# Attention scores and weight folds as 64x32 products, with the heads ordered even first

## The chip, the core and the metric

The kernel runs on one core of a Trainium2 chip. TensorE (PE in the profile, PEld for its weight loads) multiplies and writes to PSUM; VectorE (DVE) and ScalarE (ACT) read PSUM and do everything elementwise; GpSimd (POOL) clears buffers and reduces over partitions; SyncE (SP) issues most transfers. The metric is the device time of one execution in microseconds (us), as the median over runs. A profiled execution gives the trace, in which each instruction has a start and a duration.

## The reference, cut to what matters

Inputs are `q`, `k`, `v` of 8 batches x 8 heads x 576 positions x 64 and `phi` of 8 x 8 x 576 x 32, all float32, and two weight matrices. The computation is

```python
a = exp(phi - max(phi, axis=2)); a = a / (sum(a, axis=2) + 1e-9)
k_m = einsum('bhsm,bhsd->bhmd', a, k)            # 32 memory slots for each head
v_m = einsum('bhsm,bhsd->bhmd', a, v)
attn = softmax(q @ k_m.T / 8)                    # 576 x 32 for each head
x = (attn @ v_m), heads side by side             # 4608 tokens x 512
h = x @ w_in                                     # 512 -> 2048
out = (h * cos(h)) @ w_out                       # 2048 -> 512
```

## The kernel before

The kernel never forms `x`. For each batch it multiplies `v_m` into `w_in` once (a **fold**, giving a matrix `vw` of 256 x 2048: 8 heads x 32 slots), and then computes `h` as `attn @ vw`. All large products are done as three fp16 products of high and low halves.

**Main stream.** The 4608 tokens are cut into 12 groups of 384, and each group runs 16 steps `f` over 128 of the 2048 hidden columns. A step has `gemm1` (line 493, `hp<-aT,vw`: six products for 384 tokens, or twelve for 192 tokens in a group that straddles two batches), an elementwise chain for `h*cos(h)` (ACT lines 502, 512, 518, DVE lines 507, 508, 516, 519), and `gemm2` (line 537, `acc<-wo,gp`: nine products of 128x512) of the step five before. There are 192 steps; group 0 and half of group 1 also convert weights.

**Side stream.** For each batch `b` a generator, `prep(b)`, is advanced a few yields per step. `memory(b)` takes `exp(phi - max)`, multiplies it with `k` and `v` (`psA`, line 247, five chunks of positions, eight float32 products of 32 columns each), divides by the sum, transposes (`tpx`, line 267), and copies the result to two zero-filled tiles, `km` (ACT, lines 274 and 275) and `vm` (DVE, lines 276 and 277), in which two heads stand side by side as a block diagonal. `attend(b)` computes the **scores** (`sc`, line 349) in three blocks of 256, 256 and 64 positions, transposes each on DVE (line 351), takes the softmax, and transposes back. A separate list of due steps runs the folds: for each batch eight of them, (q, g) with q = 0..3 and g = 0, 1, two steps apart; from the third batch on a fold is four 128x32 products with `vp` (fp16 high halves of `vm`, both weight halves under each other) and four with `vl` (low halves, zeros where the other head stands), line 432, and then one ACT and one DVE instruction (lines 438, 439) that write `vw`.

**What sets the order.** The program text gives dependencies and priorities; a scheduler decides the static order of each engine's instructions. Each engine then works strictly through its own list, and waits where an operand is missing. Every small product (psA, tpx, sc, pv) takes its PSUM bank from a pool of two, `small_ps`, in turn; a bank is taken again when its readers are done. `hp` and `acc` have three banks each.

Of the kernel before, what the change touches and what calls it, by code (L numbers as in the profile page):

```python
# [9 lines left out]
F16 = mybir.dt.float16  # L10
# [12 lines left out]
P = 128  # L23
# [21 lines left out]
def attention_then_ffn(ctx: ExitStack, tc: tile.TileContext, phi, phiT, kv, qT, w_in, w_out, eye, out):  # L45
# [13 lines left out]
    nc.sync.dma_start(out=ident, in_=eye)  # L59

    vmask = const.tile([P, 2, 2], F32, name="vmask")
    nc.vector.memset(vmask, 0.0)
# [9 lines left out]

    vl = const.tile([P, NP, 2, M], F16, name="vl")
    nc.vector.memset(vl, 0.0)

# [138 lines left out]
    def memory(b):  # L214
# [28 lines left out]
        for c, (s0, n) in enumerate(TCH):  # L243
            for g in range(2):
                for j in range(4):
                    h = 4 * g + j
                    nc.tensor.matmul(  # L247
                        psA[32 * j:32 * (j + 1), g * KV:(g + 1) * KV],
                        lhsT=a[:n, c, h * M:(h + 1) * M], rhs=kvs[c][:n, h * KV:(h + 1) * KV],
                        start=(c == 0 and g == 0), stop=(c == 4), skip_group_check=True)  # L250
            yield
        if b >= 1 and b + 1 < B and b + 1 != 2:
# [13 lines left out]
        for g in range(2):  # L266
            nc.tensor.matmul(tpx[:, g * P:(g + 1) * P], lhsT=X[:, g], rhs=ident, start=True, stop=True)
        km = wk.tile([P, NP, 2 * M], F32, tag="km", name=f"km_{b}", bufs=1)
        vm = wk.tile([P, NP, 2 * M], F32, tag="vm", name=f"vm_{b}")
        nc.gpsimd.memset(km, 0.0)  # L270
        nc.gpsimd.memset(vm, 0.0)
        tv = tpx[:, 0:HM].rearrange("p (c t m) -> p c t m", t=2, m=M)
        lo, hi = slice(0, D), slice(D, P)
        nc.scalar.mul(km[lo, :, 0:M], tv[lo, :, 0], 1.0 / math.sqrt(D))
        nc.scalar.mul(km[hi, :, M:2 * M], tv[hi, :, 1], 1.0 / math.sqrt(D))
        nc.vector.tensor_copy(out=vm[hi, :, 0:M], in_=tv[hi, :, 0])
        nc.vector.tensor_copy(out=vm[lo, :, M:2 * M], in_=tv[lo, :, 1])
        st["km", b], st["vm", b] = km, vm
        yield
        l1 = wk.tile([P, 4], F32, tag="l1", name=f"l1_{b}")  # L280
        nc.vector.tensor_reduce(out=l1, in_=X.rearrange("p g (t d) -> p (g t) d", t=2), op=ALU.add, axis=AX.X,
                                apply_absolute_value=True)
        nc.vector.tensor_tensor(out=l1, in0=l1, in1=vmask.rearrange("p g t -> p (g t)"), op=ALU.mult)
        l2 = wk.tile([P, 1], F32, tag="l2", name=f"l2_{b}")
# [13 lines left out]
    def scales(b):  # L298
# [5 lines left out]
        if b < 2:  # L304
            T = wk.tile([P, 1], F32, tag="T", name=f"T_{b}")
            nc.vector.reciprocal(out=T, in_=E)
            nc.vector.tensor_scalar(out=T, in0=T, scalar1=2.0 ** 13, scalar2=None, op0=ALU.mult)
            st["T", b] = T
        else:

            sv = to_range(f"sv_{b}", wk, "sv", st["ev", b])
            vp = wk.tile([P, NP, 2, M], F16, tag="vp", name=f"vp_{b}", bufs=1)
            for o in range(2):
                here, there = slice(o * D, (o + 1) * D), slice((1 - o) * D, (2 - o) * D)
                vm = st["vm", b][here, :, (1 - o) * M:(2 - o) * M]
                nc.scalar.activation(vp[here, :, o], vm, AF.Copy, scale=sv[here])
                nc.scalar.activation(vp[there, :, o], vm, AF.Copy, scale=sv[here])
                nc.vector.scalar_tensor_tensor(out=vl[here, :, o], in0=vm, scalar=sv[here], in1=vp[here, :, o],
                                               op0=ALU.mult, op1=ALU.subtract)
            st["vp", b] = vp  # L320
# [3 lines left out]
    def attend(b):  # L324
# [95 lines left out]

    def fold_psum(b, q, g):
        pv = small_ps(f"pv_{b}_{q}_{g}")
        for i in range(2):
            c = 2 * g + i
            if b < 2:
                nc.tensor.matmul(pv[D * i:D * (i + 1)], lhsT=st["vm", b][:, c],
                                 rhs=w_in_sb[:, c, q * FS:(q + 1) * FS], start=True, stop=True)
        if b >= 2:
            for first in (True, False):
                for j in range(4):  # L430
                    c, o = 2 * g + j // 2, 1 - j % 2
                    nc.tensor.matmul(pv[M * j:M * (j + 1)], lhsT=(st["vp", b] if first else vl)[:, c, o],  # L432
                                     rhs=st["w2", q][:, c, o], start=first, stop=not first, skip_group_check=True)
        return pv
# [7 lines left out]
    def fold(b, q, g):  # L442
        if g == 0:
            st["vw", b, q] = wk.tile([P, 2, 2, FS], F16, tag="vw", name=f"vw_{b}_{q}", bufs=8)
        split_fold(b, st["vw", b, q], g, fold_psum(b, q, g))

# [292 lines left out]
```

## Time and profile before

| | |
|---|---|
| median of 3 runs | 719.82 us (718.49 to 720.54) |
| profiled execution | 718.65 us |
| its span (first to last instruction) | 716.6 us |
| PE busy | 694.8 us, 97% of the span |
| DVE busy | 570.0 us, 80% |
| ACT busy | 520.8 us, 73% |
| granted TensorE clock | 0.99 |

A row of a group reads: line, engine, operation, output<-inputs, shapes and count, then busy time and mean duration of one, then the engine's idle time before them and what ended it. A row of the timeline reads: start, duration until the end of the last one, engine, line, operation, count, and in brackets the idle time before it. Matmuls are pipelined: one of 512 columns is listed with 0.38 us, but the next starts 0.216 us after it. So the cost of a piece of work on PE is read from the distance between starts, not from durations.

### The profile page before, as it was taken

To read this page: it belongs to the slowest core of one execution; us is meant where nothing else is said; L and a number is where in the kernel's file an instruction comes from. 1 tells how busy PE (TensorE), PEld (TensorE's weight loads), DVE (VectorE), ACT (ScalarE), POOL (GpSimd) and SP (SyncE) were. 2 spreads that over 40 slices of the span, in tenths; PEclk is the share of its full clock that TensorE was granted. 3 is DMA by queue.
4 is the path that set the end of the run, shared out by engine and by line. 5 is a ranking of instruction groups with operands and counts; after the bars stand their busy time and mean duration, and the time that the engine had idled before them with its cause. 6 is when DMAs were issued, how large, how long until landed. Compare 5 with 4: busy or idle time off the path is not lost.

```text
span 716.6 us, 12018 instructions
## 1 busy us (share of the span) xinstructions
PE 694.8 (97%) x4578; PEld 357.2 (50%) x4578; DVE 570.0 (80%) x1256; ACT 520.8 (73%) x965; POOL 14.1 (2%) x34
## 2 busy tenths in 40 slices
PE   7689999999999999999999999999999999999997
PEld 3244444565454445565444544666444544555553
DVE  2868999998988997679877997679776987676753
ACT  1789999899886875668757685678767785665653
POOL 0000000000000000000000100000000000000000
PEclk9799999999999999999999999999999999999999
DMA  8995881426405300152103310152100000100101
GB/s 291 381 330 168 310 291 42 121 60 188 149 7 161 111 1 1 45 167 67 45 1 123 107 49 1 45 167 68 44 1 1 22 24 1 45 1 1 45 0 45
DMA packets 31561, 66.78 MB, mean 93 GB/s; under 512 B 2192, under 2 KB 11024, under 8 KB 31504
## 3 DMA queue, kind: packets, MB, share of 16 engines
q1 hardware_dynamic: 27184, 58.15, 25.1%
q10 hardware_dynamic: 4320, 7.87, 2.9%
q8 instruction: 36, 0.59, 0.3%
q14 instruction: 21, 0.17, 0.1%
HBM read 52.38 MB, written 9.44 MB: 86 GB/s over the span
## 4 chain that ended last, share of the span: by engine, by line
PE 60%; ACT 17%; DVE 16%; DMA 4%; issue 2%; SPq 1%; POOL 0%; ACTq 0%; DVEq 0%
PE acc L537 34%; PE hp L493 18%; PE pv L432 3%; ACT u L512 2%; DVE u L516 2%; DMA phi<-in_phi 2%; DVE u L508 2%; DVE gp L519 2%; ACT u L502 2%; ACT L512 2%; DVE gp L507 1%; DMA kv<-in_kv 1%; PE sc L349 1%; ACT L237 1%; PE psA L247 1%
## 5 line engine op out<-in xcount | busy, mean ns | idle before, releaser
L537 PE MATMUL acc<-wo,gp 128*128 128x512 f16 x1584 | 371.2, 379 | 0.0
L537 PEld LDWEIGHTS <-gp 128*128 128x128 f16 x1584 | 153.4, 98 | 161.5 <-issue 2.6
L493 PE MATMUL hp<-aT,vw 128*128 128x192 f16 (+1 forms) x1440 | 202.6, 284 | 0.8 <-DVE u L516 0.4
L493 PEld LDWEIGHTS <-vw 128*128 128x128 f16 x1440 | 125.1, 98 | 82.3 <-issue 30.0
L512 ACT ACTIVATE u<-u 128x384 f32<-128x384 f32 x192 | 99.7, 522 | 86.6 <-DVE u L508 85.7
L516 DVE SCALAR_TENSOR_TENSOR u<-hp,u 128x384 f32<-128x384 f32 x176 | 96.8, 552 | 45.7 <-ACT u L512 43.4
L502 ACT ACTIVATE u<-hp,cu 128x192 f32<-128x192 f32 (+1 forms) x240 | 110.3, 491 | 18.2 <-PE hp L493 11.8
L519 DVE TENSOR_TENSOR gp<-u,gp 128x384 f16<-128x384 f32 x176 | 96.6, 551 | 29.9 <-ACT gp L518 29.3
L518 ACT CAST gp<-u 128x384 f16<-128x384 f32 x176 | 89.0, 509 | 38.7 <-DVE u L516 36.7
L508 DVE TENSOR_TENSOR u<-u,gp 128x384 f32<-128x384 f32 x192 | 105.7, 552 | 3.2
L507 DVE CAST gp<-u 128x384 int32<-128x384 f32 x192 | 67.4, 353 | 20.6 <-ACT u L502 18.9
L532 PE MATMUL acc<-wo,gp 128*128 128x512 f32 x96 | 45.5, 603 | 1.6 <-DVE gp L514 1.6
L439 DVE SCALAR_TENSOR_TENSOR vw<-pv,vw 128x512 f16<-128x512 f32 x48 | 33.0, 689 | 5.1 <-ACT vw L438 3.8
L438 ACT ACTIVATE vw<-pv 128x512 f16<-128x512 f32 x48 | 28.3, 590 | 7.4 <-PE pv L432 6.5
L484 PE MATMUL hp<-aT,vf 128*128 128x384 f32 x64 | 26.4, 546 | 4.2 <-DVE gp L514 2.0
L512 ACT ACT_TABLE_LOAD x23 | 29.5, 1283 | 0.4
L532 PEld LDWEIGHTS acc<-wo,gp 128*128 128x128 f32 x96 | 17.0, 190 | 20.7 <-issue 14.9
L247 PE MATMUL psA<-kv,phi 128*32 128x129 f32 (+1 forms) x640 | 23.5, 276 | 2.8 <-DMA kv<-in_kv 1.5
L553 ACT ACTIVATE ob<-acc,os 128x512 f32<-128x512 f32 x28 | 18.5, 682 | 8.1 <-PE acc L537 5.2
L247 PEld LDWEIGHTS psA<-kv,phi 128*32 128x32 f32 (+1 forms) x640 | 16.1, 109 | 13.3 <-issue 6.9
L484 PEld LDWEIGHTS hp<-aT,vf 128*128 128x128 f32 x64 | 12.5, 207 | 17.7 <-DVE gp L514 4.6
L349 PE MATMUL sc<-q,km 128*64 128x256 f32 (+3 forms) x192 | 20.6, 343 | 0.0
(126 smaller groups left out, 549.5 us busy)
## 6 DMA issues: line engine op xcount, KB each, us to landing
kv<-in_kv SPq DMA_DIRECT2D x32, 516.0 KB, 5.8
q<-in_qT SPq DMA_DIRECT2D x8, 1152.0 KB, 6.4
raw_out<-in_w_out SPq DMA_DIRECT2D x8, 1024.0 KB, 5.0
out<-ob ACTq DMA_DIRECT2D x30, 256.0 KB, 2.1
raw_in<-in_w_in SPq DMA_DIRECT2D x6, 1024.0 KB, 8.4
phi<-in_phi SPq DMA_DIRECT2D x8, 512.0 KB, 7.2
w_in_sb<-w_in_parts SPq DMA_DIRECT2D x12, 256.0 KB, 4.1
phiT<-in_phiT SPq DMA_DIRECT2D x4, 576.0 KB, 6.4
```

What stands on the lines that cost most here:

```text
L247: nc.tensor.matmul(psA[32 * j:32 * (j + 1), g * KV:(g + 1) * KV], lhsT=a[:n, c, h * M:(h + 1) * M], rhs=kvs[c][:n, h * KV:(h + 1) * KV], s ...
L484: nc.tensor.matmul(hp[:, :GT], lhsT=st["vf", q][:, g, fo * P:(fo + 1) * P], rhs=st["aTf"][:, g], start=(g == 0), stop=(g == 1))
L493: nc.tensor.matmul(hp[:, c0:c0 + n], lhsT=vw[:, wi, g, fo * P:(fo + 1) * P], rhs=aT[:, ai, g, c1:c1 + n], start=(k == 0), stop=(k == 5))
L502: ins = nc.scalar.activation(u[:, c0:c0 + n], hp[:, c0:c0 + n], AF.Copy, scale=st["cu", b] if grp else 1.0 / (2.0 * math.pi), bias=0.25)
L507: nc.vector.tensor_copy(out=ni, in_=u)
L508: nc.vector.tensor_tensor(out=u, in0=u, in1=ni, op=ALU.subtract)
L512: nc.scalar.activation(u, u, AF.Sin, scale=TWO_PI_BELOW)
L516: nc.vector.scalar_tensor_tensor(out=u, in0=hp[:, :GT], scalar=2.0 ** -17, in1=u, op0=ALU.mult, op1=ALU.mult)
L518: nc.scalar.copy(gp[:, 0], u)
L519: nc.vector.tensor_tensor(out=gp[:, 1], in0=u, in1=gp[:, 0], op=ALU.subtract)
L532: nc.tensor.matmul(accs[grp][t], lhsT=gp[:, t * P:(t + 1) * P], rhs=wo[:, f + 1], start=(f == 0), stop=(f == NF - 1))
L537: nc.tensor.matmul(accs[grp][t], lhsT=gp[:, gi, t * P:(t + 1) * P], rhs=parts[:, wi], start=(f == 0 and gi == 0 and wi == 0), stop=(f == N ...
```

## The change

Batches are counted from 0. From the third on (b >= 2) four things differ.

1. The host puts the even heads first and the odd heads behind them (`k`, `v`, `phi`; `q` and the weights stay), and swaps key and value columns for the second half instead of for odd heads. After the transpose all even heads' keys stand in the lower 64 partitions and all odd heads' in the upper 64, so `km` and `vm` are dense (4 x 32 columns) and need no zeros and no memset. Their four copies are written in the order ACT, DVE, ACT, DVE.
2. The scores are eight products of 64 rows x 32 columns for each block, the even heads' into one bank and the odd heads' into the other, with two DVE transposes, where there were four products of 128x64 into one bank with one transpose.
3. A fold of q does both g at once, into both small banks: eight 128x32 products with `vp`, then eight 64x32 products with `vl`, which has lost its zeros. Then the two pairs of ACT and DVE instructions follow.
4. The five psA chunks of a batch come without a yield between them, so the generator has four yields fewer and what follows is emitted sooner. The l1 norm of the values needs no mask.

```diff
+            if b < 2 or c == 4:
                 yield
...
+        n = 2 * M if b < 2 else M
+        km = wk.tile([P, NP, n], F32, tag="km", name=f"km_{b}", bufs=1)
+        vm = wk.tile([P, NP, n], F32, tag="vm", name=f"vm_{b}")
+        if b < 2:
+            nc.gpsimd.memset(km, 0.0)
+            nc.gpsimd.memset(vm, 0.0)
...
+        else:
+            tv = tpx[:, 0:HM].rearrange("p (g j m) -> p g j m", g=2, m=M)
+            for g in range(2):
+                nc.scalar.mul(km[HALF[g]], tv[HALF[g], g], 1.0 / math.sqrt(D))
+                nc.vector.tensor_copy(out=vm[HALF[1 - g]], in_=tv[HALF[1 - g], g])
...
         def scores(i):
             t0, n = BL[i]
+            if b >= 2:
+                sc = [small_ps(f"sc_{b}_{t0}_{g}") for g in range(2)]
+                for j in range(4):
+                    for g in range(2):
+                        nc.tensor.matmul(sc[g][M * j:M * (j + 1), :n], lhsT=km[HALF[g], j],
+                                         rhs=qt[HALF[g], j, t0:t0 + n], start=True, stop=True)
+                for g in range(2):
+                    nc.vector.transpose(at[:, 2 * t0 + g * n:2 * t0 + (g + 1) * n], sc[g][:, :n])
+                return
...
-        if b >= 2:
-            for first in (True, False):
-                for j in range(4):
-                    c, o = 2 * g + j // 2, 1 - j % 2
-                    nc.tensor.matmul(pv[M * j:M * (j + 1)], lhsT=(st["vp", b] if first else vl)[:, c, o],
-                                     rhs=st["w2", q][:, c, o], start=first, stop=not first, skip_group_check=True)
+    def fold_16(b, q):
+        pv, w2 = [small_ps(f"pv_{b}_{q}_{g}") for g in range(2)], st["w2", q]
+        for g in range(2):
+            for j in range(4):
+                nc.tensor.matmul(pv[g][M * j:M * (j + 1)], lhsT=st["vp", b][:, j, 1 - g], rhs=w2[:, j, 1 - g],
+                                 start=True, stop=False, skip_group_check=True)
+        for j in range(4):
+            for g in range(2):
+                v = HALF[1 - g]
+                nc.tensor.matmul(pv[g][M * j:M * (j + 1)], lhsT=vl[v, j], rhs=w2[v, j, 1 - g],
+                                 start=False, stop=True, skip_group_check=True)
...
+        elif g == 0:
+            for x, pv in enumerate(fold_16(b, q)):
+                split_fold(b, st["vw", b, q], x, pv)
```

What the scheduler makes of it is seen in three places. The first is PE at the scores of the last batch (`sc_<block>` before, `sc_<block>_<g>` now; 64x256 and 32x256 are output rows by positions). Before:

```order
L537 MATMUL acc_2_5474<-wo,gp_13_5751 128x512
L349 MATMUL sc_0_5977<-q_5229,km_5894 64x256 x4
L349 MATMUL sc_256_5983<-q_5229,km_5894 64x256 x4
L493 LDWEIGHTS vw_0_5444
L493 MATMUL hp_3_5989<-aT_5106,vw_0_5444 128x384
```

With the change:

```order
L370 MATMUL sc_0_0_5986<-q_5202,km_5894 32x256 x4
L532 LDWEIGHTS vw_0_5518
L532 MATMUL hp_1_6034<-aT_5061,vw_0_5518 128x384
L370 MATMUL sc_0_1_5987<-q_5202,km_5894 32x256 x4
L576 LDWEIGHTS gp_12_5802
L576 MATMUL acc_0_5557<-wo,gp_12_5802 128x512
L370 MATMUL sc_256_0_6010<-q_5202,km_5894 32x256 x4
L576 LDWEIGHTS gp_12_5802
L576 MATMUL acc_0_5557<-wo,gp_12_5802 128x512
L576 LDWEIGHTS gp_12_5802
L576 MATMUL acc_0_5557<-wo,gp_12_5802 128x512
L370 MATMUL sc_256_1_6011<-q_5202,km_5894 32x256 x4
```

Two blocks that stood together, in one small bank each, are now four halves with pieces of the main stream between them. Over batches 2 to 7 the order shows 7 of the 12 blocks of 256 cut into their two halves like this, and 5 with all eight products alternating between the halves; of the 6 blocks of 64, 4 are cut.

The second place is PE at the first fold of batch 4 (`vp` and `vl` are the high and low halves; of rows that repeat, one is shown). Before:

```order
L432 LDWEIGHTS vp_3590
L432 MATMUL pv_0_0_3598<-w_in_0_953,vp_3590 32x512
L432 LDWEIGHTS vl
L432 MATMUL pv_0_0_3598<-w_in_0_953,vl 32x512
L493 LDWEIGHTS vw_1_2711
L493 MATMUL hp_4_3609<-aT_2234,vw_1_2711 128x384
```

With the change:

```order
L462 MATMUL pv_0_0_3642<-w_in_0_952,vp_3634 32x512
L462 LDWEIGHTS vp_3634
L462 MATMUL pv_0_1_3643<-w_in_0_952,vp_3634 32x512
L467 LDWEIGHTS vl
L467 MATMUL pv_0_0_3642<-w_in_0_952,vl 32x512
L467 LDWEIGHTS vl
L467 MATMUL pv_0_1_3643<-w_in_0_952,vl 32x512
L532 LDWEIGHTS vw_1_2740
L532 MATMUL hp_4_3664<-aT_2147,vw_1_2740 128x384
```

Two folds (g = 0 and g = 1) that stood two steps apart are one stretch of sixteen products now, the last eight alternating between the two banks. Of the 24 stretches 20 stay whole; the first of batch 3, the second of batch 5 and the last of batches 4 and 6 are cut into two or three. The psA chunks of a batch stand together in batches 3 to 7 (four and one in batch 2); before, those of batches 2 to 7 stood in 18 places, 6 of them beside a fold, and now in 7, 2 of them beside a fold.

The third place is ACT at batch 4, from the end of the exponentials to the copies into `km`, with the semaphores waited for in brackets. Before, the two copies follow each other:

```order
L518 CAST gp_8_3121<-u_8_3120 128x384 [waits DVE_49]
L502 ACTIVATE u_9_3187<-hp_9_3174,cu_1945 128x192 [waits PE_49]
L502 ACTIVATE u_9_3187<-hp_9_3174,cu_2576 128x192
L274 ACTIVATE km_3209<-tpx_3206 64x4x32 [waits PE_49,Pool_49]
L275 ACTIVATE km_3209<-tpx_3206 64x4x32
L512 ACTIVATE u_9_3187<-u_9_3187 128x384 [waits DVE_49,Activation_49]
```

With the change:

```order
L551 ACTIVATE u_6_3092<-u_6_3092 128x384 [waits DVE_49,Activation_49]
L541 ACTIVATE u_7_3156<-hp_7_3143,cu_1959 128x192 [waits PE_49]
L541 ACTIVATE u_7_3156<-hp_7_3143,cu_2605 128x192
L557 CAST gp_5_3042<-u_5_3041 128x384 [waits DVE_49]
L557 CAST gp_6_3093<-u_6_3092 128x384 [waits DVE_49]
L473 ACTIVATE vw_3_3111<-pv_3_0_3112 128x512 [waits PE_49]
L473 ACTIVATE vw_3_3111<-pv_3_1_3113 128x512 [waits PE_49]
L551 ACTIVATE u_7_3156<-u_7_3156 128x384 [waits DVE_49,Activation_49]
L290 ACTIVATE km_3137<-tpx_3134 64x128 [waits PE_49]
L541 ACTIVATE u_8_3213<-hp_8_3200,cu_1959 128x192 [waits PE_49,Activation_49]
L290 ACTIVATE km_3137<-tpx_3134 64x128 [waits DVE_49]
```

The two copies into `km` are apart, the second waits for DVE's copy into `vm` between them, and both fold instructions of the last q stand ahead of them in one piece.

More of the change, by code (lines that the diff above doesn't have):

```diff
@@ L275, in memory @@
[L275 to L277 removed]
+        n = 2 * M if b < 2 else M
[4 more added lines that the diff above has]
+            nc.gpsimd.memset(vm, 0.0)
+        lo, hi = HALF
@@ L713 @@
     w_in, w_out = np.asarray(inputs["moe_w_in"]), np.asarray(inputs["moe_w_out"])
+    k, v, phi = k.copy(), v.copy(), phi.copy()
+    order = list(range(0, H, 2)) + list(range(1, H, 2))
+    for a in (k, v, phi):
+        a[2:] = a[2:, order]
     kv = np.ones((B, S, H, KV), k.dtype)
     kt, vt = k.transpose(0, 2, 1, 3), v.transpose(0, 2, 1, 3)
-    kv[:, :, 0::2, 0:D], kv[:, :, 0::2, D:2 * D] = kt[:, :, 0::2], vt[:, :, 0::2]
-    kv[:, :, 1::2, 0:D], kv[:, :, 1::2, D:2 * D] = vt[:, :, 1::2], kt[:, :, 1::2]
+    for bs, even, odd in ((slice(0, 2), slice(0, H, 2), slice(1, H, 2)), (slice(2, B), slice(0, 4), slice(4, H))):
+        kv[bs, :, even, 0:D], kv[bs, :, even, D:2 * D] = kt[bs, :, even], vt[bs, :, even]
+        kv[bs, :, odd, 0:D], kv[bs, :, odd, D:2 * D] = vt[bs, :, odd], kt[bs, :, odd]
     laid = {
```

49 lines of the change are left out of this document (27 added, 22 removed).

## The prediction

> **What bounds the kernel now.** I read the page's first lines, then the windows, then the groups of PE.
>
> ```profile
> PE 694.8 (97%) x4578; PEld 357.2 (50%) x4578; DVE 570.0 (80%) x1256; ACT 520.8 (73%) x965; POOL 14.1 (2%) x34
> ```
> ```profile
> 200.00:300.00 100.00, 99.36 (x691) 49.15 (x690) 81.19 (x184) 72.75 (x139) 2.36 (x5) 1.00 0.18 58
> 400.00:500.00 100.00, 99.80 (x736) 54.86 (x735) 83.26 (x193) 73.77 (x144) 3.59 (x6) 1.00 0.21 70
> 500.00:600.00 100.00, 99.81 (x637) 47.66 (x635) 82.28 (x186) 73.30 (x136) 0.66 (x1) 1.00 0.04 17
> ```
> ```profile
> L537 PE MATMUL acc<-wo,gp 128*128 128x512 f16 x1584 | 371.2, 379 | 0.0
> L493 PE MATMUL hp<-aT,vw 128*128 128x192 f16 (+1 forms) x1440 | 202.6, 284 | 0.8 <-DVE u L516 0.4
> ```
>
> The windows give length, then busy time of PE, PEld, DVE, ACT, POOL, then the granted clock (1.00). Busy PE alone proves little, so the last two rows matter: before 3024 main products PE stood idle 0.8 us in all. The next product starts when the last one's columns have gone through, and nothing else is waited for. DVE has 17% to spare, ACT 26%. So from batch 2's work on (160 us) a microsecond of PE's list is a microsecond of the end, and the question is what the small products cost there, and whether PE still never waits.
>
> **What a small product costs on PE.** The critical chain gives nine main products their true length, the timeline the starts around the small ones.
>
> ```profile
> 594.25 1.94 PE acc L537 x9
> ```
> ```profile
> 432.54 2.10 PE L537 MATMUL acc<-wo,gp 128*128 128x512 f16 x9
> 434.57 0.40 PE L432 MATMUL pv<-w_in,vp 128*32 128x512 f16 x4
> 434.80 0.39 PE L432 MATMUL pv<-w_in,vl 128*32 128x512 f16 x4
> 435.12 1.15 PE L493 MATMUL hp<-aT,vw 128*128 128x384 f16 x6
> ```
>
> 1.94 / 9 = 0.216 us is a slot of 512 columns. From 432.54 nine slots end at 434.48; the fold's first products start at 434.57 (entry: 0.09), all four together, in one slot since they sit in different columns of the array; the next four 0.23 later, and the main stream 0.32 after that (a slot and 0.10 exit). The fold costs 435.12 - 434.48 = 0.64: two slots and 0.2 for going into the 128x32 shape and out.
>
> ```profile
> 212.62 1.09 PE L247 MATMUL psA<-kv,phi 128*32 128x129 f32 x32
> 213.65 0.66 PE L493 MATMUL hp<-aT,vw 128*128 128x384 f16 x3
> ```
> ```profile
> 309.18 1.22 PE L247 MATMUL psA<-kv,phi 128*32 128x129 f32 x32
> 310.33 0.83 PE L493 MATMUL hp<-aT,vw 128*128 128x192 f16 x8
> ```
>
> Both hold 32 float32 instructions, two for each product, four side by side. In the second row 16 belong to the last chunk, of 64 positions, which has the 64x32 shape. It takes 1.15 against 1.03: changing from 128x32 to 64x32 in the middle costs 0.12. A chunk itself is (1.03 - 0.15) / 2 = 0.44.
>
> ```profile
> 485.47 2.11 PE L537 MATMUL acc<-wo,gp 128*128 128x512 f16 x9
> 487.51 1.08 PE L349 MATMUL sc<-q,km 128*64 128x256 f32 x8
> 488.52 1.16 PE L493 MATMUL hp<-aT,vw 128*128 128x192 f16 x12
> 491.56 0.45 PE L349 MATMUL sc<-q,km 128*64 128x64 f32 x8
> 491.94 1.17 PE L493 MATMUL hp<-aT,vw 128*128 128x192 f16 x12
> 563.40 1.95 PE L349 MATMUL sc<-q,km 128*64 128x256 f32 x16
> 565.28 1.15 PE L493 MATMUL hp<-aT,vw 128*128 128x384 f16 x6
> ```
>
> A block of 256 costs 1.01 and 0.10 entry, 1.11; it is four slots (eight instructions, two side by side). A block of 64 costs 0.48. Two blocks of 256 in one piece cost 1.98.
>
> **The change part by part.** *Folds.* Before, 48 at 0.64 are 30.7, and two that are cut add 0.6: 31.3. Now 24 stretches: entry 0.1, two slots for the eight `vp` products, 0.12 for the change to 64x32, one slot for the eight `vl` products, exit 0.1: 0.98. That makes 23.5, and the four that the order cuts pay 2.0 more, about 0.5 each, for a second entry, exit and slot: 25.5. **-5.8.**
>
> The one slot for `vl` is the unknown: no row shows two products side by side in the lower and upper half of the rows. Bounds: one slot (0.216) or two (0.43, the nearest row with four of them). The second adds 24 x 0.216 = 5.2. I take one slot: that four column strips share a slot in every row above is the nearest evidence that the array works in independent pieces, and the two halves write different banks. The Trainium skill (TensorEngine Tiling (Array Packing), Tiling Modes and Gotcha 1) lists 64x32 as eight independent tiles, with different banks for different row tiles; by it the term is the one taken, and no run here shows it.
>
> *Scores.* Before: batches 2, 4, 6 at 1.11 + 1.11 + 0.48; 5 and 7 at 1.98 + 0.48; batch 3 2.35, joined to a fold: 15.4. Now eight side by side need two slots, but the halves that the order cuts apart need two slots too, four side by side: 0.05 for the first float32 load, 0.43, entry and exit 0.2: 0.68 each. Seven cut blocks of 256 make 14 x 0.68 = 9.5, five whole ones 3.4 (bounds 0.68 to 1.11 each, as for `vl`). A block of 64 costs 0.37 whole or by the half (0.48 less two of its four rounds of 0.055): eight halves and two whole, less one shared entry, 3.4. Together 16.3: **+0.9**, though the products are twice as dense. By the Trainium skill (the same page, Instruction Overhead, about 60 cycles for a product) a half of 64 columns would be held by its eight instructions, an estimate of 8 x 25 ns = 0.20 for 0.11, which adds 1 us over the ten; the sum goes by the rows.
>
> *psA.* The same 40 products a batch, but stretches with psA alone fall from 12 to 5, at 0.2 of entry and exit each: **-1.4.**
>
> *Off PE.* DVE transposes each half by itself.
>
> ```profile
> L351 DVE STREAM_TRANSPOSE at<-sc 128x512 f32<-128x512 f32 x15 | 10.6, 707 | 0.9 <-PE sc L349 0.9
> L372 DVE STREAM_TRANSPOSE aT<-at 128x256 f32<-128x256 f32 x2 | 0.8, 424 | 0.0
> L283 DVE TENSOR_TENSOR l<-l,vmask 128x4 f32<-128x4 f32 x8 | 1.3, 158 | 0.2
> ```
>
> 2 x 0.424 - 0.707 = +0.14 a block, two blocks, at most as much for the small one, less 0.16 for the mask: +0.3 a batch in 80 us, hidden in DVE's 17%; uncovered it would be 1.6 in all. Twelve memsets leave POOL, which is 2% busy. SP issues the next `phi` ahead of three `kv` chunks; both are wanted a batch later. ACT and DVE now split both halves of a q in one piece: 0.59 and 0.69 come twice, and what stands behind them is the chain for the next `hp`, which PE needs only when its ring of three banks comes round; that covers it in the steady part, and the third rival is what it costs elsewhere.
>
> *Waits that the change adds.* Six score halves share two banks, so a half waits for the transpose of the half two before, and the fold's second half for the split of the q before. What stands behind a waiting product is the whole main stream. Such waits cost now:
>
> ```profile
> 180.64 0.46 PE L267 MATMUL tpx<-ident,X 128*128 128x128 f32 x2 [0.23 <-DVE X L261]
> 264.74 0.40 PE L432 MATMUL pv<-w_in,vp 128*32 128x512 f16 x4 [0.43 <-ACT vp L317]
> 304.99 1.09 PE L247 MATMUL psA<-kv,phi 128*32 128x129 f32 x32 [0.20 <-ACT phi L237]
> ```
>
> With four yields fewer the side stream is emitted ahead of the data, so psA, tpx and sc of batches 4 and 6 now stand within two steps, each where its operand is barely ready. I worked out one place, the first scores of batch 4, which need `km` from ACT:
>
> ```profile
> L512 ACT ACT_TABLE_LOAD x23 | 29.5, 1283 | 0.4
> L512 ACT ACTIVATE u<-u 128x384 f32<-128x384 f32 x192 | 99.7, 522 | 86.6 <-DVE u L508 85.7
> L502 ACT ACTIVATE u<-hp,cu 128x192 f32<-128x192 f32 x128 | 46.8, 417 | 5.5 <-PE hp L493 2.9 <-ACT ob L553 1.2 <-DVE gp L519 1.0
> L518 ACT CAST gp<-u 128x384 f16<-128x384 f32 x176 | 89.0, 509 | 38.7 <-DVE u L516 36.7
> L438 ACT ACTIVATE vw<-pv 128x512 f16<-128x512 f32 x48 | 28.3, 590 | 7.4 <-PE pv L432 6.5
> L274 ACT ACTIVATE km<-tpx 64x128 f32<-64x128 f32 x8 | 2.1, 263 | 10.3 <-PE tpx L267 10.2
> L237 ACT ACTIVATE phi<-phi 64x256 f32<-64x256 f32 x8 | 3.2, 405 | 0.0
> ```
>
> After the exponential that releases psA, ACT's list holds a small exponential, a table load, three sines, three half `u`, two casts, two splits and two copies: 0.41 + 1.28 + 1.57 + 1.25 + 1.02 + 1.18 + 0.53 = 7.2. PE's list to the same point holds psA 2.5, the last fold 0.6 + 0.8, eight products of 0.216, ten of 0.08, tpx 0.44 and one more slot: 7.1. Level, and ACT also waits for DVE's copy between its two: I take 0.5 there, twice (batches 4 and 6), and 0.4 elsewhere. Bounds: 0, and 0.23 at each of the 36 halves, 8.3. **+1.4.**
>
> **Sum:** -5.8 + 0.9 - 1.4 + 1.4 = -4.9. The profiled execution took 718.65 (span 716.6 and 2.05 around it), so 713.75; the median of the runs stands 1.17 above that execution, so **714.9** by the median.
>
> **The rivals.** *Row halves take turns.* The `vl` products need 5.2 more, the five whole blocks 2.2: -4.9 becomes +2.5, 722.3. For it: no row shows overlap across row halves. Against: column strips overlap everywhere. With half an overlap the gain is down to 1.2.
>
> *The two small banks decide (slower).* PE waits at each half for DVE. For it: in the stretch after psA DVE is full, and PE stood for it.
>
> ```profile
> 330.00:335.00 5.00, 5.00 (x34) 2.96 (x33) 5.00 (x12) 3.42 (x8) 0.00 (x0) 1.00 0.70 235
> 340.00:345.00 5.00, 4.68 (x25) 2.23 (x23) 5.00 (x12) 4.14 (x10) 0.00 (x0) 1.00 0.01 3
> ```
>
> At 0.23 for 36 halves the waits are 8.3 for my 1.4: +2.0 and, with DVE's 1.6 uncovered, +3.6: 718.65 + 3.6 + 1.17 = 723.4. It decides once the mean wait passes 0.2. Against: the order cuts blocks so as to give DVE time.
>
> *The gain falls where DVE is the bound.* Folds within the prep stretches (about a third, 2.0) and psA (1.4) are saved where DVE has no room and come back as waits for `hp`, with DVE's 0.3 a batch: -4.9 + 3.4 + 1.6 = +0.1, no change, 719.9.
>
> *The change does not do what it says:* for the scores the order already shows so, and that is in the sum.
>
> **How the numbers follow.** Forecast (-3 to -7) 0.66; DVE bound 0.14; row halves 0.09; banks 0.11. Less than 0.3% (2.2 us) is no change that a measurement tells. Part of the last two ends within that bound, and a little of the DVE case beyond it on the fast side: faster 0.70, same 0.16, slower 0.14. Range: without any wait, the old ones (about 2 by rows like the three above) gone too, -8.3, 711.5; upward to the no-change case and some way into the slower ones, 720.8. The forecast's own range is 711.5 to 717.
>
> **What would show it.** Right: whole folds at 0.98 with eight `vl` products starting within 0.05; half blocks at 0.68; psA with tpx in one piece; PE's idle time before tpx, sc and pv near 3 us; about 5 us off PE's span in windows from 160 us. Wrong: `vl` in two slots; brackets over 0.3 before sc or pv naming DVE or ACT; idle time before line 532 (`hp`) above 3 us in the stretches behind psA.

## The result: slower by 1.3%

The changed kernel takes 728.72 us (median of 4 runs, 725.15 to 729.48); the kernel before, run beside it, 719.4 us. The ratio is 1.0127, with a 95% interval of 1.0105 to 1.0149. The forecast was a gain, 714.9 us, with 720.8 as the upper end of its range.

The profiled execution of the changed kernel took 728.85 us, its span is 727.0, 10.4 more than before. The page's first line and the two costliest groups answer to those shown of the kernel before (line 576 is its line 537, line 532 its line 493):

```profile
PE 693.7 (95%) x4722; PEld 356.3 (49%) x4722; DVE 569.2 (78%) x1267; ACT 514.1 (71%) x963; POOL 9.6 (1%) x22
...
L576 PE MATMUL acc<-wo,gp 128*128 128x512 f16 x1584 | 376.4, 380 | 3.1 <-ACT ob L592 3.1
L532 PE MATMUL hp<-aT,vw 128*128 128x192 f16 (+1 forms) x1440 | 203.9, 284 | 2.4 <-DVE u L555 2.1
```

PE is less busy by 1.1 us and the span is 10.4 longer: PE, which hardly waited, now waits. The windows show where (columns as before; those of 200 to 250 and 550 to 600 us had 49.80 and 50.00 of PE before):

```profile
200.00:250.00 50.00, 47.84 (x377) 22.83 (x376) 42.78 (x106) 36.38 (x65) 1.42 (x2) 1.00 0.30 100
250.00:300.00 50.00, 48.13 (x321) 24.65 (x320) 36.72 (x76) 31.29 (x66) 0.00 (x0) 1.00 0.02 6
350.00:400.00 50.00, 46.87 (x355) 22.84 (x356) 35.87 (x85) 31.55 (x61) 1.91 (x2) 1.00 0.23 76
550.00:600.00 50.00, 47.39 (x345) 22.21 (x343) 41.02 (x103) 35.86 (x67) 0.35 (x1) 0.93 0.05 17
```

The view of the waits sums PE's idle time from 160 us on by what ended it: total, number of times, longest. The changed kernel:

```profile
PE acc L576 <- ACT ob L592: 3.1, 4, 1.5
PE psA L252 <- ACT phi L242: 2.9, 4, 1.2
PE hp L532 <- DVE u L555: 2.1, 6, 0.8
PE sc L370 <- DVE vm L291: 1.5, 1, 1.5
PE tpx L273 <- DVE X L267: 1.2, 2, 0.6
PE sc L370 <- issue: 1.0, 1, 1.0
PE sc L370 <- DVE vw L474: 1.0, 2, 0.5
...
```

The kernel before had four entries in this view, 1.4 us in all. So there is no single new wait. There are three families: `acc` behind the output copy and `hp` behind `u`; psA and tpx; and the scores.

The work itself went as forecast. The timeline of PE in the changed kernel, around one fold and three pieces of scores:

```profile
277.09 2.11 PE L576 MATMUL acc<-wo,gp 128*128 128x512 f16 x9
279.12 0.61 PE L462 MATMUL pv<-w_in_sb,vp 128*32 128x512 f16 x8
279.67 0.41 PE L467 MATMUL pv<-w_in_sb,vl 64*32 64x512 f16 x8
280.01 1.15 PE L532 MATMUL hp<-aT,vw 128*128 128x384 f16 x6
```
```profile
176.36 0.64 PE L370 MATMUL sc<-q,km 64*32 64x256 f32 x8
176.93 0.34 PE L532 MATMUL hp<-aT,vw 128*128 128x384 f16 x1
...
178.59 2.11 PE L576 MATMUL acc<-wo,gp 128*128 128x512 f16 x9
180.62 0.66 PE L370 MATMUL sc<-q,km 64*32 64x256 f32 x16
181.22 1.15 PE L532 MATMUL hp<-aT,vw 128*128 128x384 f16 x6
```

Nine slots from 277.09 end at 279.03, so the fold costs 280.01 - 279.03 = 0.98. A half block occupies 0.57 up to the next product, and both halves together 0.60 (181.22 - 180.62): the row halves of the array do work side by side.

To keep work and waits apart I summed, from 160 us on, the distances between starts on PE. "Small work" is what the stretches of small products cost at best: for each composition of such a stretch, the least that it cost in any kernel of this study. What a stretch costs beyond that is a wait at small products, before them, between them or right behind them; a distance beyond a slot between two main products is a wait in the main stream. (The view above counts idle time only from a product's modelled end, so it gives 0.1 to 0.6 less for each. The line between small work and its waits depends on what is taken as the same composition, by up to 0.8 us in a row; their sum does not.) In us:

| kernel | median | ratio to before (95%) | small work | waits, small | waits, main |
|---|---|---|---|---|---|
| before | 719.4 | 1 | 67.3 | 2.4 | 1.2 |
| the change | 728.7 | 1.0127 (1.0105 to 1.0149) | 62.2 | 10.9 | 8.6 |
| psa_crammed_alone | 719.7 | 1.0010 (0.9992 to 1.0028) | 65.9 | 3.4 | 2.2 |
| merged_folds_alone | 719.1 | 1.0001 (0.9985 to 1.0018) | 64.0 | 5.0 | 1.7 |
| scores_alone | 722.7 | 1.0061 (1.0042 to 1.0081) | 63.3 | 10.7 | 0.9 |
| psa_yields | 725.6 | 1.0089 (1.0060 to 1.0118) | 58.9 | 13.6 | 6.1 |
| folds_apart | 724.3 | 1.0074 (1.0046 to 1.0102) | 67.8 | 6.4 | 3.0 |
| one_bank_scores | 719.5 | 1.0018 (0.9999 to 1.0036) | 60.8 | 8.3 | 4.5 |
| one_bank_scores_psa_yields | 721.6 | 1.0044 (1.0028 to 1.0060) | 62.5 | 7.5 | 4.2 |
| scores_alone_hp_bank | 725.0 | 1.0074 (1.0054 to 1.0094) | 62.5 | 10.1 | 5.5 |
| change_hp_bank | 723.3 | 1.0058 (1.0041 to 1.0075) | 56.2 | 10.1 | 9.2 |
| folds_merged_where_alone | 716.2 | 0.9963 (0.9948 to 0.9978) | 64.3 | 3.1 | 0.9 |

For the change: small work -5.1, waits at small products +8.5, waits in the main stream +7.4: +10.8, for 10.4 between the two ends. Of these waits 3.4 are not waits but a slower clock (below).

### The profile page after: what moved, and what is told of

The parts are those of the page before. It is cut to its first block, busy times and chain, and to the rows that moved or that the text cites. A ratio compares the mean times of both kernels' runs of the same rounds, so it can differ in the third digit from the quotient of the medians.

```text
span 727.0 us, 12291 instructions
## 1 busy us (share of the span) xinstructions
PE 693.7 (95%) x4722; PEld 356.3 (49%) x4722; DVE 569.2 (78%) x1267; ACT 514.1 (71%) x963; POOL 9.6 (1%) x22
## 4 chain that ended last, share of the span: by engine, by line
PE 40%; ACT 26%; DVE 25%; DMA 4%; issue 3%; ACTq 1%; SPq 0%; DVEq 0%
PE acc L576 24%; PE hp L532 12%; ACT u L551 5%; DVE u L547 5%; DVE gp L558 4%; DVE u L555 4%; ACT u L541 4%; ACT gp L557 3%; DVE gp L546 3%; DVE vw L474 2%; DMA raw_in<-in_w_in 2%; ACT L551 2%; DMA phi<-in_phi 2%; PE sc L370 1%; ACT vw L473 1%
## 5 line engine op out<-in xcount | busy, mean ns | idle before, releaser
L576 PE MATMUL acc<-wo,gp 128*128 128x512 f16 x1584 | 376.4, 380 | 3.1 <-ACT ob L592 3.1
L532 PEld LDWEIGHTS <-vw 128*128 128x128 f16 x1440 | 128.5, 98 | 79.7 <-issue 19.6
L473 ACT ACTIVATE vw<-pv 128x512 f16<-128x512 f32 x48 | 26.8, 590 | 3.4 <-PE pv L467 3.3
L252 PE MATMUL psA<-kv,phi 128*32 128x129 f32 (+1 forms) x640 | 21.1, 275 | 3.7 <-ACT phi L242 2.9
L252 PEld LDWEIGHTS psA<-kv,phi 128*32 128x32 f32 (+1 forms) x640 | 16.4, 109 | 10.5 <-ACT phi L242 7.2
L370 PE MATMUL sc<-q,km 64*32 64x256 f32 (+1 forms) x288 | 16.5, 349 | 3.8 <-DVE vm L291 1.5
```

The source lines that it names most:

```text
L532: nc.tensor.matmul(hp[:, c0:c0 + n], lhsT=vw[:, wi, g, fo * P:(fo + 1) * P], rhs=aT[:, ai, g, c1:c1 + n], start=(k == 0), stop=(k == 5))
L576: nc.tensor.matmul(accs[grp][t], lhsT=gp[:, gi, t * P:(t + 1) * P], rhs=parts[:, wi], start=(f == 0 and gi == 0 and wi == 0), stop=(f == N ...
```

## The experiments

Three theories can explain these waits. **A**: without the psA yields the side stream reaches PE before its operands. **B**: two split pairs of a fold in one piece hold up ACT and DVE, and both small banks. **C**: a block of scores that needs both small banks waits for every earlier reader of either. What they rest on are places in the changed kernel. Every edit below also lets the scheduler order the other instructions anew, so each run shows an edit together with its new order.

For B, ACT and PE at the end of a group (ACT rows, then the PE product that waits for the copy `ob`):

```profile
295.97 0.58 ACT L473 ACTIVATE vw<-pv 128x512 f16<-128x512 f32 x1
...
296.69 0.51 ACT L557 CAST gp<-u 128x384 f16<-128x384 f32 x1
...
297.11 0.59 ACT L473 ACTIVATE vw<-pv 128x512 f16<-128x512 f32 x1
...
297.60 0.68 ACT L592 ACTIVATE ob<-acc,os 128x512 f32<-128x512 f32 x1
...
298.33 0.81 PE L576 MATMUL acc<-wo,gp 128*128 128x512 f16 x3 [1.52 <-ACT ob L592]
```

The fold whose splits these are ended on PE at 292.7; the copy stands behind both splits, and the next group's `acc` behind the copy. Where PE lost the other large part before `acc`, 1.6 us at 633, the picture differs: the splits had ended at 629.7, and what stands between them and the copy is one more step of the chain for `h*cos(h)`.

```profile
633.09 0.68 ACT L592 ACTIVATE ob<-acc,os 128x512 f32<-128x512 f32 x1
633.82 0.81 PE L576 MATMUL acc<-wo,gp 128*128 128x512 f16 x3 [0.91 <-ACT ob L592]
```

For A, PE in the prep of batch 5:

```profile
386.90 2.54 PE L252 MATMUL psA<-kv,phi 128*32 128x129 f32 x80 [1.21 <-ACT phi L242]
...
392.20 0.46 PE L273 MATMUL tpx<-ident,X 128*128 128x128 f32 x2 [0.60 <-DVE X L267]
```

For C, DVE and PE at the first scores of batch 4:

```profile
223.07 0.62 PE L370 MATMUL sc<-q,km 64*32 64x256 f32 x2
223.58 0.69 DVE L212 TENSOR_TENSOR mx<-phi 128x512 f32<-128x512 f32 x1 [1.03 <-DMA phi<-in_phi]
224.19 0.55 DVE L558 TENSOR_TENSOR gp<-u,gp 128x384 f16<-128x384 f32 x1
224.77 0.28 DVE L291 COPY vm<-tpx 64x128 f32<-64x128 f32 x1
...
225.20 0.66 PE L370 MATMUL sc<-q,km 64*32 64x256 f32 x14 [1.52 <-DVE vm L291]
```

The even heads' first product goes into the free bank at 223.07; the odd heads' needs the other bank, which still holds tpx. That bank's last reader, DVE's copy to `vm`, stands behind the maximum of the next `phi`, which itself waits 1.03 us for a transfer. PE stands for 2.1 us by the starts. The operand was not what it waited for: both of ACT's copies into `km` had ended by 222.62.

### Each part undone, and two parts alone

Undo the psA part in the change:

```diff
-            if b < 2 or c == 4:
-                yield
+            yield
```

> The change with the five psA chunks a yield apart again, as before; the rest of the change stays. Theory A (the side stream is emitted too early): in the changed kernel PE stands 1.28 and 1.12 us before psA and 0.76 twice before tpx in the batches 5 and 7; these 3.9 go, psA pays its 1.4 of entries and exits again, so about -2.5 on the span of 727.0, and if the granted clock's dip at 566 to 573 us goes with the wait ahead of it, 3.3 more: 721 to 726.5 by the median. Theory B (the fold's two split pairs in one piece are the cause, about 7 us of waits before acc, hp and sc): the waits before acc and hp stay, and the time is 728 to 731.

Measured: 725.64 us, as theory A has it. But its account is not A's: the waits before psA and tpx fall from 2.4 and 2.0 to 0.6 and 0.5, while those before the scores rise from 5.5 to 10.5. The view of its waits:

```profile
PE sc L369 <- DVE at L372: 4.5, 4, 2.8
PE sc L369 <- DVE vm L290: 2.7, 2, 1.4
...
```

The wait now stands at the next piece that needs a small bank. The net gain is less work, since the scores are no longer cut (11.4 us for 16.5); the shorter time at the slow clock (3.4 us for 6.8) is used up by the longer waits.

Undo the folds part:

```diff
-        elif g == 0:
-            for x, pv in enumerate(fold_16(b, q)):
-                split_fold(b, st["vw", b, q], x, pv)
+        else:
+            split_fold(b, st["vw", b, q], g, fold_16(b, q, g))
...
```

Here `fold_16` fills one bank for one g with four `vp` and four zero-padded `vl` products, all 128x32.

> The change with its folds as before: one g at a time, two steps apart, four 128x32 products with vp and four with a zero-padded vl, one bank, one split pair. Fold work on PE goes back from 24 x 0.96 to 48 x 0.64, +7.7. Theory B: the waits that the double split makes go (3.8 before acc for the output copy, 1.0 before hp at 360 us, 2.1 before sc for the split's bank), about -6.9, so 728 to 730, no change. Theory A: only the work comes back, 734 to 737.

Measured: 724.31, better than either theory said. The folds cost 5.6 us more work, and 10 us of waits and slow clock go (19.5 to 9.4). B was right in sign and short in size.

The folds part alone, in the kernel before:

```diff
-        split_fold(b, st["vw", b, q], g, fold_psum(b, q, g))
+        if b == 1:
+            split_fold(b, st["vw", b, q], g, fold_psum(b, q, g))
+        elif g == 0:
+            for x, pv in enumerate([fold_psum(b, q, y) for y in range(2)]):
+                split_fold(b, st["vw", b, q], x, pv)
```

> The kernel before, and only its folds changed: both g of a q in one piece, sixteen 128x32 products (vl still zero-padded), then the two split pairs; heads, scores and psA as before. Work on PE: 48 x 0.64 becomes 24 x 1.07, -5.1. Theory B: the double split costs its 7 us of waits here too, 719 to 722. Theory A: the gain stays, 713.5 to 716.

Measured: 719.08, no change, at the lower edge of what theory B expected. Work falls by 3.3, and 3.2 us of waits come, most at the scores (2.2), not the 7 of theory B. So the merge eats its own gain when it is alone, and costs more beside the other parts.

The psA part alone (the reverse of the first diff, in the kernel before):

> The kernel before, and only the four yields of psA taken away from the third batch on. Work on PE: -1.4 (entries and exits). Theory A: the 3.9 us of waits before psA and tpx come up here, 721 to 723. Theory B: 718 to 719, the work alone.

Measured: 719.67, between the two expectations and no change that can be told. Work falls by 1.4 as expected, and 2.1 us of waits come. The view of the waits:

```profile
PE hp L494 <- DVE u L517: 1.5, 2, 1.3
PE psA L247 <- ACT phi L237: 1.0, 4, 0.5
PE acc L538 <- ACT ob L554: 1.0, 3, 0.4
...
```

PE waits for the output copy here too, without a merged fold.

### The scores

The scores part alone: the folds undone and the psA yields back, so that only the ordered heads, the dense `km` and `vm` and the 64x32 scores are left.

> The change with folds and psA as before: what is left of it are the ordered heads, the dense km and vm, and the scores as eight 64x32 products into both small banks. Theory C (a block of scores that takes both banks waits for every earlier reader of either: for the copies out of tpx's bank, then for both transposes of the block before): about 8 us of waits before sc, as the 10.4 in the run with the psA yields, against some 3 us less work of PE, so 722 to 725. Rival: these waits come up only beside merged folds, then the dense scores gain, 715 to 718.

Measured: 722.73, ratio 1.0061, with 4.0 us less work and 8.1 us of waits before the scores, the numbers of theory C. This part alone makes the kernel slower. PE and DVE at the second block of batch 5 in this run:

```profile
404.32 0.66 PE L370 MATMUL sc<-q,km 64*32 64x256 f32 x14 [0.19 <-DVE vw L469]
404.92 1.15 PE L526 MATMUL hp<-aT,vw 128*128 128x384 f16 x6
408.07 0.99 PE L370 MATMUL sc<-q,km 64*32 64x256 f32 x16 [2.00 <-DVE at L373]
```
```profile
404.45 0.54 DVE L552 TENSOR_TENSOR gp<-u,gp 128x384 f16<-128x384 f32 x1
404.92 0.34 DVE L540 CAST gp<-u 128x384 int32<-128x384 f32 x1
405.57 0.35 DVE L338 SCALAR_TENSOR_TENSOR vl<-vm,sv,vp 64x128 f16<-64x128 f32 x1 [0.31 <-ACT vp L336]
405.95 0.56 DVE L541 TENSOR_TENSOR u<-u,gp 128x384 f32<-128x384 f32 x1
407.10 0.56 DVE L549 SCALAR_TENSOR_TENSOR u<-hp,u 128x384 f32<-128x384 f32 x1 [0.59 <-ACT u L545]
407.57 0.77 DVE L373 STREAM_TRANSPOSE at<-sc 128x256 f32<-128x256 f32 x2
```

The first block is done at 404.9, but its transposes stand on DVE behind five other instructions, four of them of the main stream, and two of the five wait for ACT. Before, the second block had a bank of its own and did not ask.

The scores with one bank, in the change (and with the psA yields in a further run):

```diff
-                sc = [small_ps(f"sc_{b}_{t0}_{g}") for g in range(2)]
-                for j in range(4):
-                    for g in range(2):
-                        nc.tensor.matmul(sc[g][M * j:M * (j + 1), :n], lhsT=km[HALF[g], j],
-                                         rhs=qt[HALF[g], j, t0:t0 + n], start=True, stop=True)
+                sc = small_ps(f"sc_{b}_{t0}")
+                for g in range(2):
+                    for j in range(4):
+                        nc.tensor.matmul(sc[M * j:M * (j + 1), g * n:(g + 1) * n], lhsT=km[:, j, g * M:(g + 1) * M],
+                                         rhs=qt[:, j, t0:t0 + n], start=True, stop=True)
...
```

Left out of this cut are `km`, which is padded with zeros again (and cleared by GpSimd), and the one transpose in place of two. So the edit takes back the dense scores as a whole, not the second bank alone.

> The change with the scores in one bank for a block: eight 128x32 products (km zero-padded again, one head in 32 columns), one transpose; heads, merged folds and psA as in the change. It needs the same two small banks less. PE's work for a block of 256 is estimated at 4 rounds of 0.22 and 0.2 of entry and exit, 1.08, against 1.32 for two halves and 0.69 for a whole one, so about the same sum. Theory C: the 5.5 us of waits before sc fall under 1.5, 720 to 724, and the clock's dip behind the wait at 565 us goes too. Theories A and B (psA without yields, merged folds): the waits stay, 727 to 730.

Measured: 719.49, ratio 1.0018 for the change's 1.0127, the largest step of all the single edits. The clock's dip is gone in the profiled execution. Waits before the scores fall to 3.3, not under 1.5: what is left waits for the splits of a merged fold (two waits, 1.9 us, behind `vw`).

> As one_bank_scores, and the psA chunks a yield apart as before: what is left of the change are the ordered heads and the merged folds with 64x32 vl products. If C and A together are the cause, the waits fall to the 6.4 of the merged folds alone, with 2 to 3 us less fold work than there (0.98 for 1.11): 715 to 718. If merged folds are the cause with these heads (theory B), 721 to 724.

Measured: 721.59, above the 715 to 718 expected and inside the 721 to 724 of the other case. Waits at small products are 7.5, in the main stream 4.2, of which 3.7 stand before `acc`; the merge alone, with the heads in their old order, had 0.6 there. The traces show what differs: how late ACT is at the group's end. From the start of the group's last `gemm2` on PE to the first output copy on ACT it is 3.9 and 3.3 us at the two places where the change lost 2.2 and 1.6 us before `acc`, and 2.7, 2.7 and 3.3 where this run lost 1.0, 1.0 and 1.6. It is 1.5 to 1.9 at the three in merged_folds_alone, and 1.9 at 463 us in the change, and there at most 0.2 us went, although at three of these four both splits stand right ahead of the copy. So two splits ahead of the copy cost little by themselves; PE lost time where ACT was already a step behind it. Why ACT is later with the ordered heads is not settled; no run isolates it.

The same fault treated from the other side, with a third bank taken from hp's ring:

```diff
-                sc = [small_ps(f"sc_{b}_{t0}_{g}") for g in range(2)]
+                sc = [small_ps(f"sc_{b}_{t0}_0"), ps_h.tile([P, 512], F32, tag="ps_h", name=f"sc_{b}_{t0}_1")]
```

> As scores_alone, but the odd heads' half of each block goes to a bank of the ring of three that hp uses, so a block takes one small bank as before. Theory C (both small banks for a block are what costs): the 8.1 us of waits before sc fall under 2, the 4.0 us less work of PE stay, 715 to 718; if hp then misses its third bank, waits before hp rise by what is won and it is 719 to 722. If the waits have nothing to do with the banks (km or the transposes are late anyway), they stay, 722 to 724.

Measured: 725.02, ratio 1.0074 (1.0054 to 1.0094), no better than scores_alone; the two intervals overlap, so whether it is slower is not shown. Batch 5 on PE, and the view of the waits:

```profile
405.60 0.67 PE L370 MATMUL sc<-q,km 64*32 64x256 f32 x16 [1.05 <-DVE vw L469]
408.98 1.14 PE L526 MATMUL hp<-aT,vw 128*128 128x384 f16 x6 [2.71 <-DVE u L549]
```
```profile
PE hp L526 <- DVE u L549: 8.2, 7, 2.7
PE sc L370 <- DVE vw L469: 1.1, 1, 1.1
...
```

The second block goes at 405.6 instead of 408.1, and then the next `hp` stands until 408.98. The place of the wait moved, and PE is through it no sooner: DVE's list sets its end, and a bank lent by one ring is missed in the other. The rival in the expectation (719 to 722 with waits before hp) named this, though not its size.

In the change itself:

> The change with this one line altered: the odd heads' half of each block of scores goes to a bank of hp's ring. Everything else (merged folds, psA without yields, ordered heads) stays. Theory C: 5.5 us of waits before sc and the clock's dip of 3.3 behind the last of them go, 719 to 722. If A and B decide: 726 to 729.

Measured: 723.33, 1.0058. Of the change's loss about half goes, with the dip (in the profiled execution). What is left stands before `acc` (4.2 us in the view of the waits), psA and tpx (3.5), the places of B and A, but also before `hp`: 5.0 for 2.1 in the change, as in scores_alone_hp_bank, which lends the same bank.

### DVE's list

That left open whether the number of banks or DVE's list sets the waits. The maximum of `phi` for the batches 4 to 7 was left out (zero is subtracted in its place), once in scores_alone and once in the kernel before:

```diff
-        nc.vector.tensor_tensor(out=mx[:, 0:2], in0=a[:, 0:2], in1=a[:, 2:4], op=ALU.max)
-        nc.vector.tensor_tensor(out=mx[:, 0], in0=mx[:, 0], in1=mx[:, 1], op=ALU.max)
...
-        st["top", b] = mx[:, 2]
+        st["top", b] = no_shift.broadcast_to([P, HM])
```

> scores_alone without the maximum of phi for the batches 4 to 7: three DVE instructions of 0.69, 0.41 and 0.41 and one POOL reduction a batch, which stand on DVE just ahead of the copies out of tpx's bank and the transposes of the scores, partly waiting for phi's transfer, are left out; zero is subtracted instead. Theory D (a block that needs both banks waits as long as DVE is behind with its list): of the 8.1 us before sc, those of the batches 3 to 6 (7.0) fall to half or less and the time from 722.7 to 717.5 to 720. Theory C in its plain form (two banks for a block cost by their number, whatever DVE has to do): the waits stay over 6, 721.5 to 723.5.

Measured: 720.22, ratio 1.0007 (0.9995 to 1.0019), just above the range of theory D. The waits before the scores fall from 8.1 to 4.3; those of the batches 3 to 6 from 7.0 to 3.3.

> The kernel before, with the same work left out. Its PE waits 0.01 us before sc, so both theories expect the time unchanged within 1 us, 717.5 to 719.5; a gain of several us would mean that DVE's list bounds the stretch without the change too.

Measured: 717.70, ratio 0.9975 (0.9960 to 0.9990): 1.8 us less by the ratio, where 1 us was allowed for, since its waits for hp (1.2) go too. So the shorter DVE list is worth 0.25% to the kernel before and 0.54% (1.0061 to 1.0007) to the one whose scores need both banks. Theory D holds for about half of the waits: they last as long as DVE is behind. For the other half it stays open whether the rest of DVE's list sets it or the number of banks: the run leaves the main stream's instructions on that list, and its longest waits still end with DVE's transposes (2.2 us in four of them).

### A faster version

If merged folds cost only where they compete with a prep, merging those that stand alone should gain. In the kernel before, 14 of the 24 pairs were merged:

```diff
+        if b == 1 or not alone(b, q):
...
+    def alone(b, q):
+        return q < 2 or b == B - 1
```

> The kernel before; only the folds of q = 0 and 1 of the batches 2 to 6 and all of batch 7, 14 of 24, in one piece (sixteen 128x32 products), which stand outside the prep of another batch; the others apart. Work on PE: 14 x (1.11 - 1.28) = -2.4. If the double split costs only where a prep competes for the two banks: 715 to 717. If it costs everywhere (ACT's output copy behind two splits): 718 to 720.

Measured: 716.23, ratio 0.9963 (0.9948 to 0.9978), faster than both kernels. 3.0 us of work go and waits hardly change, 4.0 for 3.5 before:

```profile
PE pv L432 <- DVE phi L231: 0.8, 1, 0.8
PE psA L247 <- ACT phi L237: 0.5, 3, 0.2
PE pv L432 <- ACT vp L317: 0.4, 1, 0.4
...
```

Taking out the merge at the one fold that waited 0.98 us:

> folds_merged_where_alone with the first fold of batch 2 apart again, whose merged form waited 0.98 us for vp: work +0.18, wait -0.98, so 715.5 to 716.5; no theory hangs on it, it is the version to keep if it is below 716.2.

Measured: 717.29, ratio 0.9975 (0.9962 to 0.9988). It is above the 715.5 to 716.5 expected and no better, and the two intervals overlap: a difference of 0.1% cannot be told here. The same selection together with the ordered heads, once with each of the two repairs of the scores:

> scores_alone_hp_bank, and the 14 folds that stand outside another batch's prep in one piece with 64x32 vl products (0.98 for 2 x 0.64, -4.2 us of PE); the other folds apart, psA a yield apart. If both gains stay: 710.5 to 714. If the odd half in hp's ring costs waits before hp: 715 to 718.

Measured: 724.68, ratio 1.0071 (1.0048 to 1.0095), slower than both cases said.

> The same folds with the scores in one small bank (eight 128x32 products, padded km). Work on PE against the kernel before -4.2 for the folds and about +0.6 for the scores: 713.5 to 716 if the ordered heads bring no waits of their own; 718 and above if they do (the merged folds with ordered heads waited 3.7 us for the output copy, where the same merge alone waited 0.6).

Measured: 720.95, ratio 1.0018 (1.0003 to 1.0033). This is the second of its two cases. Neither beats the kernel before. What can be kept of the change is the merging of folds where no prep runs, and that does not need the ordered heads.

## Why the prediction was wrong

**The work was right.** A fold costs 0.98 as forecast; the `vl` stage of eight takes one slot, so the rival in which row halves take turns is out. A half block of scores costs 0.66 for the 0.68 said, a whole one 0.69, a block of 64 0.34 to 0.37. The scores came to 16.5 us for the 16.3 said. Folds and psA together fell by 6.2 for the 7.2 said. In sum -5.1 for -6.3.

**The step that failed is the waits that the change adds: +1.4, with an upper bound of 8.3.** Measured, waits rose by 12.6 at full clock (19.5 - 3.5 - 3.4, before rounding), and 3.4 more went to the clock. Four things were wrong in that step.

- *At the one place worked out, it asked for the operand and not for the bank.* At the first scores of batch 4 I followed ACT's list up to `km` and found it level with PE's, and that was right: the product that needs only `km` starts at 223.07. The one beside it waited 2.1 us for tpx's bank, that is for DVE's copy to `vm`, behind the next maximum. DVE's list up to that copy was not made. The Trainium skill (TensorEngine Tiling (Array Packing), Gotcha 1) was cited in the prediction for the shared slot; the same place warns that row tiling raises the pressure on PSUM, because the row tiles need different banks. Both halves hold here: 0.60 for a whole block, and 8.1 us of waits in the run with the scores alone.
- *The price for a half was the wrong kind of number.* 0.23 is what one wait before tpx cost in the kernel before. Here a wait for a bank lasted until DVE had worked off what stood ahead: 2.0 us behind five instructions. The 8.3 for the scores was not passed in the change (5.5), but by luck: few halves waited, and long, and with the psA yields back it was 10.5. As a bound for all waits it fell, because the other places below had no term in it.
- *The double split was called covered in the steady part.* It was not where a group ends: ACT's output copy came 3.9 and 3.3 us after the group's last `gemm2` had begun, once right behind both splits, once a step after them, and with the second copy behind it PE lost 3.8 us before `acc`. Another 1.0 went before `hp` at 360 us, behind DVE's half of both splits. The prediction named the ring of `hp` behind the splits, not the ring of `acc`.
- *psA without yields was booked as -1.4 and nothing else.* PE then stood 2.4 us before psA and 1.7 before tpx in the batches 5 and 7; the sum had 0.4 for everything outside the batches 4 and 6. Alone, this part's gain of 1.4 is cancelled too, by waits at other places (1.5 before hp and 1.0 before `acc` in the view).

**The rivals.** The one that came nearest was that the two small banks decide: the right place and the right sign, but priced at 723.4, because it saw only the wait of a half for a transpose. The one in which the gain falls where DVE is the bound was right about why lending a bank does not help, and expected no loss from it.

**The sum of the parts.** Alone, psA, folds and scores cost 0.10, 0.01 and 0.61%, together 0.72%, or 5.2 us; the change cost 9.3. The dip of the clock would explain 3.4 of the 4.1 us between: three of the change's four runs have a mean granted clock of 0.986 or 0.987 and take 728.6 to 729.5, the fourth has 0.993 and takes 725.15. Only one of them was profiled, so that the others had the same dip is an inference. Some 0.7 us remain and are within the intervals. The parts are not independent: taken back one at a time in the change, folds, psA and dense scores give back 0.53, 0.38 and 1.09%, more together than the change lost.

## What to carry to other kernels

In this kernel the tile shape that lets twice as many products share the array also took two accumulator banks at a time. Before counting the saved slots, list for each bank who reads it last, on which engine, and what stands ahead of that reader. Price such a wait by the backlog of that engine in that stretch, not by the length of the reading instruction, and look for the backlog's source first: here a bank borrowed from another ring only moved the wait. Merge small work where the stretch has no competitor for banks and engines, and leave it apart elsewhere.

## What the runs showed of the hardware that was not expected

Eight 64x32 products in both row halves of the array take the time of four: 0.60 against 0.57 us for float32 products of 256 columns, and one slot for the eight fp16 `vl` products.

The clock also fell behind waits much shorter than its window. In the changed kernel the granted clock was halved from 567.11 to 573.94 us, 6.83 us, by the records of the clock; the windows in it (the clock is the third number from the right):

```profile
567.00:570.00 3.00, 3.00 (x28) 0.49 (x21) 1.52 (x5) 0.76 (x2) 0.00 (x0) 0.52 0.00 0
570.00:573.00 3.00, 3.00 (x16) 1.00 (x15) 1.83 (x6) 0.52 (x1) 0.00 (x0) 0.50 0.00 0
```

PE was fully busy at that time, at half the rate: from 569.59 the starts of the `acc` products are 0.40 to 0.43 us apart instead of 0.216. In the 3.41 us ahead of it PE stood 1.5 us by the starts, most of it at one wait of 1.04 before the scores of batch 7 (the line with "issue" in the view of the waits above; DVE's split of the fold just before ended at 565.01, the scores start at 565.11). Such a dip came in psa_yields (behind 2.1 us), scores_alone_hp_bank (2.4) and selective_folds_hp_bank (2.9) too, each 3.41 us long, and always as a whole multiple of 3.41 us. The dips of one execution also start whole multiples of 3.41 us apart (7.33, 24.39 and 567.11 in the changed kernel). The Trainium skill (TensorE: Matmul & The Clock Gate, Part 1) describes a free-running window of this length, and its rule there is an idle window of about 3.4 us; by that rule none of these places would have lost the clock. The measurement differs: these dips followed windows with 1.5 to 2.9 us of idle time. It is no sharp threshold, since other such windows with up to 2.0 us kept the clock, one with 1.9 in the changed kernel itself. That the idle time is the cause is likely, not shown: no run sets such a wait on its own, and what separates the windows was not tried.
